# The first item's absolute value on VectorE, and a second scratch buffer for the row maxima

## The chip, the core and the metric

The kernel runs on one core of a Trainium2 chip. A core has five engines, each with its own queue, in order: TensorE (PE, matmuls; its weight loads are listed as PEld), VectorE (DVE), ScalarE (ACT), GpSimd (POOL) and SyncE (SP, which issues most DMAs). The engines wait for each other by semaphores. The metric is the device time of one execution in microseconds (us); lower is better.

## The reference

The input x has 2048 rows of 448 numbers. The output mixes two branches by a gate computed from each row of x:

```python
x = A_u
g = _sigmoid((x * gate_w).sum(-1, keepdims=True))
a = _A_ref(x, ...)     # a long convolution and a skip
b = _B_ref(x, ...)     # attention in 4 segments, 16 heads, with a memory
return g * a + (1 - g) * b
```

The convolution's kernel K is a sum over 256 states of decaying complex exponentials, for each of 448 channels and 2048 positions, and the convolution itself goes through Fourier transforms:

```python
A = -jnp.exp(log_A_real) + 1j * A_imag
C = (C_real + 1j * C_imag) * dt[:, None]
P = jnp.exp((A * dt[:, None])[:, :, None] * pos[None, None, :])
K = 2.0 * jnp.einsum("dn,dnl->dl", C, P).real
```

The attention works in segments of 512 rows, masks what lies ahead of the query, and takes the softmax of the scaled logits; for that each row's maximum is needed:

```python
logits = jnp.einsum("bhqd,bhkd->bhqk", qs, ks) * scale + mask
p = _softmax(logits, axis=-1)
```

## The kernel before

Two halves follow each other. The **first half** builds the convolution's kernel (`first_half`), and beside it projects x to queries, keys and values and transforms x. The **second half** (`second_half`) does the attention, the convolution in the Fourier domain and the output.

In the first half the 448 channels are 28 blocks of 16, and each block has two items, n = 0 to 55. Four items make a group; the groups are numbered 0 to 13 here. For each item:

- `turns(n)`: eight matmuls on TensorE write an angle, in turns, to the PSUM tile `ps_arg` (128x1024; two buffers). These are the rows `ps_arg<-ct,lh` and `ps_arg<-mag,one`.
- `trig(n)`: ScalarE reads that angle twice, once by `Sin` into one half of the tile `cs` and once by `Abs` into the other half; a second `Sin` with a bias then turns the absolute value into the cosine, in place.
- `product(n)`: VectorE multiplies these with decays: X (L392) needs the cosine, Y (L396, L397, L398) the sine.
- `sums(n)`: 64 small matmuls on TensorE add the products up in `ps_k`; after four items VectorE copies `ps_k` to `kb` (L419).

After a group's fourth item come `decays`: six exponentials on ScalarE for the next group (EY and EX, from matmuls `ps_arg<-ce,lh`). Sine and exponential need different function tables, so ScalarE loads a table twice in each group (ACT_TABLE_LOAD). From a sine table load to the next exponential one is called a sine stretch here.

The work beside it, the **feed**, is a generator of steps: matmuls `ps_m<-xh,w` (projections), `ps_m<-wvh,xh` (values), `ps_m<-ut,s1u` (transform of x) and others, with their copies `hi`, `lo`, `am`, `pkT`, `v`, `gs` on ScalarE or VectorE. `feed.spend(us)` issues steps until their stated costs reach the given time; what is over or missing is carried on. A group's rate stands in `RATES`; an item spends 1.7 times the rate, and the places among the six exponentials spend `PLACE` times it. While the exponentials run, the feed's copies are made on VectorE, else on ScalarE. In the sine stretches and beside them VectorE and ScalarE keep the order in which the code issues their main operations (`k.strict`, `follow`); TensorE keeps its program order throughout.

In the second half there are 16 blocks of four heads. For each, `maxima(i)` goes through six steps: matmuls write logits to `ps_mx` (one buffer of 128x2x512), and VectorE then runs `tensor_tensor_reduce`, which adds the mask `mk` and takes the maximum of a row. It writes the masked logits to a scratch tile `jk` that nobody reads, and the maximum, by a short instruction that reads the accumulator, to `mx`. A step has two or four of these, 16 in a block, 256 in all. `jk` had one buffer; the tile `rcb` in `divide` has the same tag, thus the same memory.

What sets the order around both places, in a few lines:

```python
        if n % 4 < 3:
            turns(n + 1)
        trig(n)
        feed.spend(1.7 * RATES[n // 4])
        product(n)
        if n % 4 > 0:
            sums(n - 1)
        if n % 4 == 3 and n + 1 < 2 * NJ:
            decays(n // 4 + 1)
            turns(n + 1)
```

Of the kernel before, what the change touches and what calls it, by code (L numbers as in the profile page):

```python
# [12 lines left out]
F32 = mybir.dt.float32  # L13
F32R = mybir.dt.float32r
BF16 = mybir.dt.bfloat16
I32 = mybir.dt.int32
AF = mybir.ActivationFunctionType
ALU = mybir.AluOpType
# [9 lines left out]
SEG = 512  # L28
# [279 lines left out]
def first_half(nc, k, gy, feed):  # L308
# [4 lines left out]
    act, v = k.act, nc.vector  # L313
# [16 lines left out]
    def load(J):  # L330
        if J < NJ:
            load_decay(J)
            load_phase(J)
# [26 lines left out]
    def turns(n):  # L360

        J, c = divmod(n, 2)
        arg[n] = pt = k.ps("arg")
        for nt in range(2):
            r, kw = rows(nt)
            k.mm(pt[:, nt], lt[J][r, c], k.ct[r, 0], start=True, stop=False, **kw)
        for i in range(2):
            for nt in range(2):
                r, kw = rows(nt)
                k.mm(pt[:, nt], k.one[r], k.mag[r, i : i + 1].broadcast_to([64, 512]), start=False, stop=False, **kw)  # L370
        for nt in range(2):
            r, kw = rows(nt)
            k.mm(pt[:, nt], lt[J][r, c], k.ct[r, 1], start=False, stop=True, **kw)

    def trig(n):

        pt = arg.pop(n)
        cs[n] = t = gw.tile([128, 2, 2, 2, 256], F32, tag="cs", name="cs", bufs=2)
        pv = pt.rearrange("p t (w c) -> p t w c", w=2)
        act(t[:, 1].rearrange("p w t c -> p t w c"), pv, AF.Sin, scale=TWO_PI)  # L380
        act(t[:, 0].rearrange("p w t c -> p t w c"), pv, AF.Abs)
        fl = t[:, 0].rearrange("p w t c -> p (w t c)")
        act(fl, fl, AF.Sin, bias=k.bhp, scale=-TWO_PI)

# [36 lines left out]
    def decays(g):  # L421
        for J in (2 * g, 2 * g + 1):
            for blk in range(3):
# [3 lines left out]
                if g > 0:  # L427
                    k.exps = 3 * (J % 2) + blk >= 2
                    feed.spend(PLACE[3 * (J % 2) + blk] * RATES[g])
                    k.exps = False  # L430
# [7 lines left out]
    for n in range(2 * NJ):  # L438
        if n < 4:
            load(n + 2)  # L440
        elif n % 2 == 0:
            load(n // 2 + 4)
        if n % 4 < 3:
            turns(n + 1)
        trig(n)
        feed.spend(1.7 * RATES[n // 4])
        product(n)
        if n == 2 * NJ - 1:
            feed.fill(2)
# [5 lines that stand above are left out]
# [3 lines left out]

PLACE = (1.24, 0.62, 0.62, 0.62, 0.0, 0.62)

RATES = (1.65, 1.65, 1.24, 1.55, 1.55, 1.17, 1.17, 1.48, 1.55, 1.17, 1.17, 1.48, 1.48, 1.65)


class Feed:
# [482 lines left out]
def attend(nc, k, ap):  # L947

    v, act = k.dve, k.sca.activation
# [32 lines left out]
    def maxima(i):  # L982


        q, kk = Q[i], K[i]
        mx = ap.tile([128, 4, 4], F32, tag="mx", name="mx", bufs=2)
        for b, hp in MSTEPS:
            pt = k.ps("mx")
            for t, o, n in PLACES[b]:
                qt = 3 - t  # L990
                for x in range(2):
                    h = 2 * hp + x
                    r = slice(32 * h, 32 * h + 32)
                    k.mm(
                        pt[:, x, o : o + n], q[r, 0, 128 * qt : 128 * qt + 128], kk[r, 0, :n],
                        start=True, stop=True, tile_position=(32 * h, 0),
                    )
            for t, o, n in PLACES[b]:
                for x in range(2):
                    h = 2 * hp + x  # L1000
                    junk = ap.tile([128, SEG], F32, tag="jk", name="jk", bufs=1)
                    v.tensor_tensor_reduce(
                        junk[:, :n], pt[:, x, o : o + n], k.mk[:, SEG - n :], 1.0, -3e38,
                        ALU.add, ALU.max, mx[:, h, 3 - t : 4 - t],
                    )
            yield
        yield
        pm = k.ps("m")
        k.tr(pm[:16, :128], mx.rearrange("p h t -> p (h t)"), k.ident)
        mn = ap.tile([16, 128], F32R, tag="mn", name="mn", bufs=2)  # L1010
        act(mn, pm[:16, :128], AF.Copy, scale=-1.0)
        k.pdma(
            q[:, 0].rearrange("(j e) (t c) -> e j t c", e=32, c=128)[28].bitcast(F32),
            mn.bitcast(F32),
        )
        yield
# [174 lines left out]
    def divide(hg):  # L1191

        o = pvss[3][:, hg]
        pb = k.ps("m")
        k.mm(pb, k.den, o, start=True, stop=True)
        rc = ap.tile([128, SEG], F32, tag="jk", name="rcb", bufs=1)
        x = None
        for h in range(2):
            c = slice(256 * h, 256 * h + 256)
            with k.issue_after(x.ins) if x else ExitStack():  # L1200
                v.reciprocal(rc[:, c], pb[:, c])
            v.scalar_tensor_tensor(o[:, c], o[:, c], k.omg[:, hg : hg + 1], rc[:, c], ALU.mult, ALU.mult)
            x = v.tensor_tensor(o[:, c], o[:, c], am[3][:, hg, c], ALU.add)
# [461 lines left out]
```

## Time and profile before

| | us |
|---|---|
| three runs | 852.44, 861.59, 861.74 |
| their median | 861.59 |
| the profiled execution | 857.84 |
| its span, first to last instruction | 855.5 |

The span is what the profile's times are counted in, from its start. Engine rows in the profile give the start, the time, the engine, the line (of a helper, where one records all operations: L1377 and L1423), the operation, output<-input, and in brackets how long the engine sat idle before it and what ended this. A wait row gives who waited for whom: us in total, times, longest. A group row gives busy time in all, mean ns of one, and the idle time before. TensorE's ends are modelled, so its busy time is an upper bound of its work. The granted clock of TensorE was 0.946 of full speed in the mean.

### The profile page before, as it was taken

The numbers are of one execution on the slowest core, as the hardware profiler recorded it, in microseconds if no ns is written. First come the engines' busy times: TensorE is split into PE (matmuls) and PEld (weight loads), VectorE is DVE, ScalarE is ACT, GpSimd is POOL, SyncE is SP. The second block draws the span as 40 slices with busy tenths as digits, with TensorE's granted clock in tenths as the row PEclk, the third lists the DMA queues.
The fourth block names the chain that finished last, engine by engine and source line by source line (L and its number), as shares of the span: only waits on it lengthen the run. The fifth ranks groups of instructions, "written<-read, shape, count | busy, mean of one in ns | idle before, by whom it ended". The sixth has DMA issues, their size and how long they took to land.

```text
span 855.5 us, 19160 instructions
## 1 busy us (share of the span) xinstructions
PE 720.8 (84%) x7678; PEld 393.9 (46%) x7703; DVE 581.3 (68%) x1139; ACT 519.6 (61%) x626; POOL 157.2 (18%) x193
## 2 busy tenths in 40 slices
PE   1687988998989988799987787879988798878897
PEld 1364655764556655566643343334433344333333
DVE  8878678867787577976675556558556765662564
ACT  4877889798988899998862144445236333430220
POOL 5324111011100111001100021123114113220110
PEclk9998999998989999999996699999999999988999
DMA  9347853325642346314558769675849577535883
GB/s 247 90 111 240 238 185 111 97 92 164 199 131 79 124 143 206 134 51 143 185 190 290 271 214 277 208 263 155 317 157 317 181 239 239 173 121 225 208 247 117
DMA packets 92450, 157.84 MB, mean 185 GB/s; under 512 B 23074, under 2 KB 60442, under 8 KB 92362
## 3 DMA queue, kind: packets, MB, share of 16 engines
q1 hardware_dynamic: 88410, 153.91, 55.7%
q10 hardware_dynamic: 3072, 1.84, 0.8%
q8 instruction: 61, 1.00, 0.5%
q0 software_dynamic: 880, 0.87, 0.3%
q14 instruction: 27, 0.22, 0.1%
HBM read 88.38 MB, written 60.24 MB: 174 GB/s over the span
## 4 chain that ended last, share of the span: by engine, by line
PE 49%; DVE 17%; ACT 16%; issue 8%; DMA 6%; SPq 2%; POOL 1%; DVEq 0%; ACTq 0%; POOLq 0%
PE ps_m L1423 15%; PE ps_pv L1423 8%; PE ps_c L1423 7%; ACT cs L1377 7%; PE ps_w L1423 6%; DVE jk L1377 6%; PE ps_mx L1423 5%; PE ps_arg L1423 4%; PE ps_k L1423 3%; DVE Y L396 2%; ACT L1377 2%; PE ps_m L1426 2%; DVE pr L1377 2%; DVE Y L397 1%; DMA winv<-in_B_wv 1%
## 5 line engine op out<-in xcount | busy, mean ns | idle before, releaser
L1377 DVE CUSTOM_DVE_ANT_0 jk<-ps_mx,mk 128x512 f32<-128x512 f32 (+3 forms) x256 | 125.4, 490 | 81.5 <-PE ps_mx L1423 72.7
L1377 ACT ACTIVATE PT<-ps_w 128x1024 f32<-128x1024 f32 (+1 forms) x96 | 84.6, 881 | 151.5 <-PE ps_w L1423 150.7
L358 POOL TENSOR_TENSOR EX<-EX,cab 128x1024 f32<-128x1024 f32 x28 | 53.9, 1928 | 311.1 <-ACT EX L1377 267.6
L1377 ACT ACTIVATE cs<-ps_arg 128x1024 f32<-128x1024 f32 x111 | 107.3, 1021 | 3.0 <-DVE Y L397 2.5
L1423 PE MATMUL ps_m<-xh,w 112*128 112x512 f32 x256 | 92.8, 412 | 1.0 <-DMA w<-WD 0.5
L1045 POOL TENSOR_SCALAR_AFFINE_SELECT PT<-PT 128x256 f32<-128x256 f32 (+1 forms) x96 | 46.6, 485 | 243.5 <-ACT PT L1377 243.4
L1423 PE MATMUL ps_w<-qu,ku 32*128 32x512 f32 (+3 forms) x768 | 87.1, 344 | 2.8 <-ACT PT L1377 2.5
L392 DVE TENSOR_TENSOR X<-EX,cs 128x1024 f32<-128x1024 f32 x56 | 70.7, 1262 | 24.9 <-ACT cs L1377 24.7
L1423 PE MATMUL ps_k<-Y,X 128*32 128x64 f32 x3584 | 64.8, 227 | 10.7 <-DVE Y L397 10.7
L1423 PE MATMUL ps_mx<-ku,qu 32*128 32x512 f32 (+3 forms) x256 | 47.6, 409 | 30.1 <-DVE mx L1377 27.7
L1423 PEld LDWEIGHTS ps_k<-Y,X 128*32 128x32 f32 x3584 | 55.5, 114 | 37.8 <-DVE Y L397 17.7
L396 DVE TENSOR_TENSOR Y<-EY,cs 128x1024 f32<-128x1024 f32 x56 | 69.1, 1234 | 0.0
L1423 PEld LDWEIGHTS ps_w<-qu,ku 32*128 32x128 f32 x768 | 60.0, 186 | 13.2 <-issue 6.1
L1377 ACT ACTIVATE cs<-cs,bhp 128x1024 f32<-128x1024 f32 x56 | 64.4, 1151 | 1.8
L1377 ACT ACTIVATE EY<-ps_arg 128x1024 f32<-128x1024 f32 x52 | 53.2, 1030 | 12.9 <-PE ps_arg L1423 11.8
L398 DVE SCALAR_TENSOR_TENSOR Y<-EY,cs 128x512 f32<-128x512 f32 x56 | 40.5, 723 | 29.6 <-ACT cs L1377 29.0
L1423 PEld LDWEIGHTS ps_m<-xh,w 112*128 112x128 f32 x256 | 48.0, 188 | 20.3 <-issue 7.7
L1423 PEld LDWEIGHTS ps_mx<-ku,qu 32*128 32x128 f32 x256 | 22.6, 193 | 70.6 <-DVE mx L1377 51.9
L1423 PE MATMUL ps_pv<-wz 128*128 128x512 bf16 x137 | 48.4, 407 | 3.6 <-ACT pvs L1377 3.1
L1423 PE MATMUL ps_m<-xl,w 112*128 112x512 f32 x128 | 50.2, 392 | 0.0
L1423 PE MATMUL ps_arg<-ct,lh 64*128 64x512 bf16 x224 | 43.0, 389 | 8.1 <-ACT cs L1377 5.7
L1423 PEld LDWEIGHTS <-lh 64*128 64x128 bf16 x392 | 21.8, 95 | 51.2 <-issue 38.6
(215 smaller groups left out, 1324.7 us busy)
## 6 DMA issues: line engine op xcount, KB each, us to landing
w<-WD SPq DMA_DIRECT2D x32, 448.0 KB, 4.4
qu<-QD SPq DMA_DIRECT2D x16, 512.0 KB, 5.6
ku<-KD SPq DMA_DIRECT2D x16, 512.0 KB, 9.9
GU<-gs SPq DMA_DIRECT2D x32, 224.0 KB, 3.4
GK<-gs SPq DMA_DIRECT2D x8, 896.0 KB, 4.6
gk<-GK SPq DMA_DIRECT2D x16, 448.0 KB, 4.5
gu<-GU SPq DMA_DIRECT2D x16, 448.0 KB, 3.7
ks<-ks SPq DMA_DIRECT2D x32, 224.0 KB, 4.3
```

The lines of the kernel that those rows point to most:

```text
L358: nc.gpsimd.tensor_tensor(o, o, cab, ALU.mult)
L392: v.tensor_tensor(X, ex, t[:, :, 0], ALU.mult)
L396: v.tensor_tensor(Y[:, :, :, :32], lo, y[:, :, :, ::-1], ALU.mult)
L397: v.tensor_tensor(Y[:, 0, :, 32:], ey[:, :, 32:], y[:, 0], ALU.mult)
L398: v.scalar_tensor_tensor(Y[:, 1, :, 32:], ey[:, :, 32:], -1.0, y[:, 1], ALU.mult, ALU.mult)
L1045: nc.gpsimd.affine_select(sl, sl, pat, ALU.is_ge, 0.0, base=0, channel_multiplier=-1)
L1377: x = op(*args, **kw)
L1423: tc.keep_in_program_order(nc.tensor.matmul(*args, **kw))
L1426: tc.keep_in_program_order(nc.tensor.transpose(*args))
```

## The change

The absolute value of each group's first item (n % 4 == 0) is made on VectorE: the sign bit is masked off by a bit operation on the angle in PSUM, and VectorE's instruction is issued ahead of ScalarE's sine. The other three items keep `Abs` on ScalarE. The feed is dealt anew: the fourth item of a group spends 2.5 times the rate where the others spend 1.7, and the rates are other numbers. The scratch tile `jk` gets two buffers, and so does `rcb`, which shares its tag.

```diff
@@ trig
         pv = pt.rearrange("p t (w c) -> p t w c", w=2)
+        if n % 4 == 0:
+            v.tensor_scalar(
+                t[:, 0].rearrange("p w t c -> p t w c").bitcast(I32), pv.bitcast(I32), 0x7FFFFFFF, None, ALU.bitwise_and
+            )
         act(t[:, 1].rearrange("p w t c -> p t w c"), pv, AF.Sin, scale=TWO_PI)
-        act(t[:, 0].rearrange("p w t c -> p t w c"), pv, AF.Abs)
+        if not (n % 4 == 0):
+            act(t[:, 0].rearrange("p w t c -> p t w c"), pv, AF.Abs)
         fl = t[:, 0].rearrange("p w t c -> p (w t c)")
         act(fl, fl, AF.Sin, bias=k.bhp, scale=-TWO_PI)
@@ the loop over items
-        feed.spend(1.7 * RATES[n // 4])
+        feed.spend(ITEMS[n % 4] * RATES[n // 4])
@@ the tables
+ITEMS = (1.7, 1.7, 1.7, 2.5)
+
-RATES = (1.65, 1.65, 1.24, 1.55, 1.55, 1.17, 1.17, 1.48, 1.55, 1.17, 1.17, 1.48, 1.48, 1.65)
+RATES = (1.65, 1.58, 1.19, 1.49, 1.49, 1.12, 1.2, 1.42, 1.45, 1.12, 1.12, 1.42, 1.32, 1.47)
@@ maxima
-                    junk = ap.tile([128, SEG], F32, tag="jk", name="jk", bufs=1)
+                    junk = ap.tile([128, SEG], F32, tag="jk", name="jk", bufs=2)
@@ divide
-        rc = ap.tile([128, SEG], F32, tag="jk", name="rcb", bufs=1)
+        rc = ap.tile([128, SEG], F32, tag="jk", name="rcb", bufs=2)
```

How it moves instructions is seen at three places. The line numbers after the change are 5 higher in and behind `trig`, and 7 higher further down (L1377 becomes L1384). The first place is ScalarE's queue where group 4 begins, before (each row: line, operation, output<-input, and in brackets the queues whose semaphores it waits for):

```order
L1377 ACTIVATE EX<-ps_arg 128x1024 [waits DVE_49,PE_49,Pool_49]
L1377 ACT_TABLE_LOAD
L1377 ACTIVATE cs<-ps_arg 128x2x2x256 [waits PE_49]
L1377 ACTIVATE cs<-ps_arg 128x2x2x256
L1377 ACTIVATE cs<-cs,bhp 128x1024 [waits Activation_49]
L1377 ACTIVATE v_207<-ps_m 128x16x28 [waits PE_49]
```

The same place of ScalarE's queue after the change:

```order
L1384 ACTIVATE EX<-ps_arg 128x1024 [waits DVE_49,PE_49,Pool_49]
L1384 ACT_TABLE_LOAD
L1384 ACTIVATE cs<-ps_arg 128x2x2x256 [waits DVE_49]
L1384 ACTIVATE cs<-cs,bhp 128x1024
L1384 ACTIVATE v_207<-ps_m 128x16x28 [waits PE_49]
```

The absolute value is gone from ScalarE. The sine, which waited for TensorE, now waits for VectorE (for the absolute value, which itself waits for TensorE), and the cosine no longer waits for a result of ScalarE.

The second place is VectorE's queue at the start of group 5, before (`gs` are the feed's copies of transformed x, `kb` the copy of the finished sums, `lo` and `ph` parts of a projection):

```order
L788 SCALAR_TENSOR_TENSOR ph<-ps_m,e 128x512
L775 SCALAR_TENSOR_TENSOR lo<-ps_m,po,hi 128x512
L1377 COPY gs<-ps_m 128x448 x2
L419 COPY kb<-ps_k 128x8x64
L398 SCALAR_TENSOR_TENSOR Y<-EY,cs 128x16x32
L392 TENSOR_TENSOR X<-EX,cs 128x1024
```

The same place of VectorE's queue after the change:

```order
L795 SCALAR_TENSOR_TENSOR ph<-ps_m,e 128x512
L782 SCALAR_TENSOR_TENSOR lo<-ps_m,po,hi 128x512
L1384 COPY gs<-ps_m 128x448
L424 COPY kb<-ps_k 128x8x64
L1384 COPY gs<-ps_m 128x448
L381 TENSOR_SCALAR cs<-ps_arg 128x2x2x256
L403 SCALAR_TENSOR_TENSOR Y<-EY,cs 128x16x32
L397 TENSOR_TENSOR X<-EX,cs 128x1024
```

The absolute value stands ahead of the first product, and one of the two `gs` copies has moved behind `kb`, just ahead of it. Groups 9 and 10 show the same move.

The third place is VectorE's queue at the start of group 6, before (`am` is a copy of what is recalled from the memory):

```order
L1377 COPY gs<-ps_m 128x448 [waits DMAHW4_49,PE_49]
L1377 COPY gs<-ps_m 128x448 [waits DMAHW6_49,PE_49]
L419 COPY kb<-ps_k 128x8x64 [waits PE_49]
L398 SCALAR_TENSOR_TENSOR Y<-EY,cs 128x16x32 [waits Activation_49]
L392 TENSOR_TENSOR X<-EX,cs 128x1024 [waits Activation_49,Pool_49]
```

The same place of VectorE's queue after the change:

```order
L1384 COPY gs<-ps_m 128x448 [waits DMAHW7_49,PE_49]
L424 COPY kb<-ps_k 128x8x64 [waits PE_49]
L1384 COPY am<-ps_m 128x512 [waits PE_49]
L381 TENSOR_SCALAR cs<-ps_arg 128x2x2x256 [waits PE_49]
L403 SCALAR_TENSOR_TENSOR Y<-EY,cs 128x16x32 [waits Activation_49]
L397 TENSOR_TENSOR X<-EX,cs 128x1024 [waits DVE_49,Activation_49,Pool_49]
```

Here a copy `am`, which ScalarE made before, has come to VectorE, between `kb` and the absolute value, and X now waits for VectorE's own absolute value too. In the second half the order of VectorE, ScalarE, GpSimd and TensorE is as before, and so are the names of the semaphores that the maxima wait for: each of the 160 that follow another directly waits for one of VectorE's own results, with one buffer for that of the maximum just ahead, with two for the one before it.

## The prediction

> **What bounds the kernel now.** I read the page's busy times and its chain first, then a table of windows cut at ScalarE's table loads, then the timeline at the points where the edits act, and last the waits.
>
> ```profile
> PE 720.8 (84%) x7678; PEld 393.9 (46%) x7703; DVE 581.3 (68%) x1139; ACT 519.6 (61%) x626; POOL 157.2 (18%) x193
> PE 49%; DVE 17%; ACT 16%; issue 8%; DMA 6%; SPq 2%; POOL 1%; DVEq 0%; ACTq 0%; POOLq 0%
> ```
>
> No engine bounds the whole: half of the chain is TensorE, and VectorE and ScalarE share a third. So each stage needs its own look. In the first half (to about 444 us) every group of four items begins with a sine stretch, from the sine table load to the exponential one. Five such stretches (columns: length, then busy us of each engine, then granted clock, DMA share, GB/s):
>
> ```profile
> core 0: us, PE busy (x) PEld busy (x) DVE busy (x) ACT busy (x) POOL busy (x), PEclk, DMA share, GB/s
> 144.55:159.77 15.22, 14.10 (x204) 10.22 (x200) 11.69 (x17) 14.36 (x16) 1.91 (x1) 1.00 0.09 18
> 174.66:189.61 14.95, 14.62 (x195) 9.85 (x195) 10.72 (x14) 14.79 (x16) 1.91 (x1) 1.00 0.39 129
> 200.44:217.51 17.07, 15.21 (x182) 9.44 (x181) 11.79 (x15) 15.36 (x17) 1.91 (x1) 0.80 0.30 102
> 227.41:244.51 17.10, 15.23 (x182) 9.35 (x181) 11.78 (x15) 15.37 (x18) 1.91 (x1) 0.80 0.41 138
> 312.39:327.70 15.31, 12.27 (x182) 7.55 (x181) 11.45 (x15) 15.15 (x18) 1.91 (x1) 1.00 0.33 106
> ```
>
> In group 9 (312.39) ScalarE is busy 15.15 of 15.31 us and TensorE only 12.27: ScalarE bounds it. In group 4 (174.66) both are full, 14.79 and 14.62 of 14.95, so less ScalarE work alone would hardly shorten it. Group 5 (200.44) has the same 182 matmuls as group 9, but at a granted clock of 0.80 it takes 1.76 us longer; group 6 (227.41) likewise. VectorE has 3 to 4 us free in each.
>
> **Edit 1: the first item's absolute value on VectorE.** The start of group 4:
>
> ```profile
> 173.25 1.03 DVE L419 COPY kb<-ps_k 128x512 f32<-128x512 f32 x1 [2.44 <-PE ps_k L1423]
> 174.00 0.38 PE L1423 MATMUL ps_arg<-ct,lh 64*128 64x512 bf16 x2
> 174.66 1.28 ACT L1377 ACT_TABLE_LOAD   x1
> 175.96 1.94 ACT L1377 ACTIVATE cs<-ps_arg 128x1024 f32<-128x1024 f32 x2
> 177.93 1.15 ACT L1377 ACTIVATE cs<-cs,bhp 128x1024 f32<-128x1024 f32 x1
> 179.18 1.23 DVE L392 TENSOR_TENSOR X<-EX,cs 128x1024 f32<-128x1024 f32 x1 [1.47 <-ACT cs L1377]
> L1377 ACT ACTIVATE cs<-ps_arg 128x1024 f32<-128x1024 f32 x111 | 107.3, 1021 | 3.0 <-DVE Y L397 2.5
> ```
>
> Sine and Abs are the pair at 175.96, the cosine starts at 177.93, 1.97 us behind the sine. The pair takes 1.94 us and one of them 1.02 us, so an independent second one starts 0.92 us behind the first. After the change the cosine follows the sine without a wait on ScalarE itself (the order shows none), so I put it 0.92 us behind: 1.05 us less on ScalarE in each group. ScalarE also gets a new wait: the sine stands behind VectorE's absolute value. Queued behind that sine are the cosine, the copies am, pkT or v, and the next item. So the gain is 1.05 us less the lateness of the sine.
>
> The absolute value reads 128x1024 from PSUM; VectorE did not do that before. Nearest rows:
>
> ```profile
> L1377 DVE COPY gs<-ps_c 128x896 f32<-128x896 f32 x8 | 8.7, 1091 | 15.5 <-PE ps_c L1423 10.4 <-issue 4.6 <-PE ps_mx L1423 0.5
> L1377 DVE COPY gs<-ps_m 128x448 f32<-128x448 f32 x13 | 8.0, 619 | 2.7 <-PE ps_m L1423 2.7
> ```
>
> 472 ns for 448 more columns is 1.05 ns a column; 128 more than 896 give 1.23 us. Bounds: 1.09 us (the 896 row) below and 2.46 us (half that speed, a bit operation being unseen here) above; I take 1.23, nearest to the copies. A handover is 0.10 us (the cosine ends at 179.08, X starts at 179.18). So VectorE needs to be free, and the first angle ready, 1.33 us ahead of the sine's old start. In group 4 both are so by 174.38 (173.25 + 1.03, and 174.00 + 0.38), 1.58 us ahead: hidden behind the table load. Elsewhere a copy stands later on VectorE:
>
> ```profile
> 117.09 0.68 DVE L1377 COPY pkT<-ps_m 128x512 f32<-128x512 f32 x1
> 118.91 1.94 ACT L1377 ACTIVATE cs<-ps_arg 128x1024 f32<-128x1024 f32 x2
> 144.44 0.67 DVE L1377 COPY pkT<-ps_m 128x512 f32<-128x512 f32 x1
> 145.84 1.94 ACT L1377 ACTIVATE cs<-ps_arg 128x1024 f32<-128x1024 f32 x2
> 199.03 1.03 DVE L419 COPY kb<-ps_k 128x512 f32<-128x512 f32 x1 [0.65 <-PE ps_k L1423]
> 201.74 1.94 ACT L1377 ACTIVATE cs<-ps_arg 128x1024 f32<-128x1024 f32 x2
> 256.48 0.69 DVE L1377 COPY am<-ps_m 128x512 f32<-128x512 f32 x1
> 257.84 1.94 ACT L1377 ACTIVATE cs<-ps_arg 128x1024 f32<-128x1024 f32 x2
> 89.41 0.69 DVE L773 TENSOR_TENSOR lo<-ps_m,hi 128x512 fp32r<-128x512 f32 x1
> 90.16 1.94 ACT L1377 ACTIVATE cs<-ps_arg 128x1024 f32<-128x1024 f32 x2
> ```
>
> Group 2: 117.77 + 1.33 is 0.19 us late, gain 0.86. Group 3: 145.11 + 1.33, 0.60 late, gain 0.45. Groups 7 and 11 (row of 7): 257.17 + 1.33, 0.66 late, gain 0.39 each. In groups 5, 9 and 10 the new order puts one gs copy (0.62 us) behind kb: 200.06 + 0.62 + 1.33, 0.27 late, gain 0.78 each. Group 6 gets an am copy (0.69 us) there: gain about 0.71. Together 5.1 us. Groups 4 and 8: 1.05 us on ScalarE, but TensorE idles only 0.33 us there: 0.4 us each, 0.8 together. Group 1: 90.10 + 1.33 is 1.27 late, a loss of 0.2 us. Groups 0, 12 and 13 I have not worked out (other work stands ahead of the sine there); they and group 1 are set to zero together. Term: 5.9 us. Bounds: 14 x 1.05 = 14.7 us; at an absolute value of 2.46 us, a loss of about 5 us.
>
> The Trainium skill, "PSUM — Partial Sum Buffer", section "Terms", says that no two engines may access the same bank in the same partition at once, reads among them. The order agrees with that page, since the sine waits for VectorE; without that wait the eight groups would give 8 x 1.05 = 8.4 us and not 5.1.
>
> **The feed dealt anew.** TensorE's matmuls are the same. With ITEMS and RATES a group is dealt 11.32 times its rate, against 10.52 before: in group 1 17.9 and not 17.4 us. The order shows few steps that change their stretch: parts of six or three matmuls go from before a sum to behind it, values matmuls go behind the last exponent, one projection part (six matmuls) goes from group 12 into 13. TensorE is in order, so this moves work within the same TensorE time: nothing. SP's issues of GU, ut and lh change places with it; by the code most are issued a group ahead of their use, and if that cover were gone TensorE would wait as here:
>
> ```profile
> 441.56 2.30 PE L1423 MATMUL ps_m<-ut,s1u 64*128 64x448 f32 x4 [0.81 <-DMA ut<-in_A_u]
> ```
>
> At this end of the first half the order has one transform step and two ut loads fewer left: 0.8 us gained, between 0 and 2.
>
> **Edit 2: two buffers for jk.** In the second half VectorE:
>
> ```profile
> 716.37 0.69 DVE L1377 CUSTOM_DVE_ANT_0 jk<-ps_mx,mk 128x512 f32<-128x512 f32 x1
> 716.99 0.08 DVE L1377 DVE_READ_ACCUMULATOR2_ANT mx<- 128x1 f32 x1
> 717.10 0.69 DVE L1377 CUSTOM_DVE_ANT_0 jk<-ps_mx,mk 128x512 f32<-128x512 f32 x1
> 717.72 0.08 DVE L1377 DVE_READ_ACCUMULATOR2_ANT mx<- 128x1 f32 x1
> 717.72 0.74 DVE L1377 SCALAR_TENSOR_TENSOR am<-am,gh,ps_m 128x512 f32<-128x512 f32 x1
> ```
>
> The second jk starts 0.11 us behind the read of the accumulator (716.99 to 717.10), while the am operation, which writes elsewhere, starts with such a read (both 717.72). With one buffer each later maximum waits for the write of the one ahead; with two it waits for the one before that, long done. So 0.11 us goes per maximum that follows another directly. There are 160 of these (10 in each of 16 blocks), 17.6 us of VectorE's time; what counts is where the chain passes through them and on to TensorE:
>
> ```profile
> PE ps_mx L1423 <- DVE mx L1377: 27.7, 25, 2.5
> 459.99 0.69 DVE jk L1377
> 767.83 0.29 DVE jk L1377
> ```
>
> The chain holds 68 such followers, these two the first and the last: 68 x 0.11 = 7.5 us. Some of it meets a TensorE that waits for another operand next, so I take three quarters, 5.6 us; bounds 0 and 17.6. The buffer rcb only shares the tag; its two reciprocals write halves of one tile: nothing.
>
> **Sum.** 5.9 + 0.8 + 5.6 = 12.3 us. The profiled execution took 857.84 us (span 855.5): 845.5. The three runs (852.44, 861.59, 861.74) and this one have a mean of 858.4, 0.6 above it, and the median shown lies 3.75 above it. I add 0.6: 846 us.
>
> **Rivals.** (a) *The wait of jk costs nothing by itself*: the 0.11 us is the maximum's own end, and the next one needs it with any buffer. For it: no row shows two maxima without the wait. Against it: the am operation at 717.72. The second term falls away: 852 us. The Trainium skill, "VectorE: DVE Perf Modes", section "The DRAIN you can't avoid", measured eight copies with and without semaphores at the same time and says the semaphore costs nothing extra. By that page this rival holds; the two starts at 717.72 speak against the page.
>
> (b) *The absolute value comes too late*: VectorE's copies wait for TensorE in more groups than here, and the first term is nil. For it: 0.60 and 0.66 us of lateness already; against it: groups 2, 4 and 8. 857.84 - 6.4 + 0.6 = 852 us.
>
> (c) *More comes*: the waits of TensorE behind the first cosine shrink, and the slow clock of groups 5 and 6 does not appear. The 1.76 us between the two windows above, twice, and the full 7.5 us: 857.84 - 5.9 - 0.8 - 3.5 - 7.5 + 0.6 = 841 us.
>
> (d) *Slower*: the absolute value takes 2.46 us. The eight groups then lose 8 x 0.59 = 4.7 us in place of gaining 5.1; TensorE waits at the same place, and groups 9 and 10 get the clock of group 5, 3.5 us; with (a) that gives 867 us. It decides at 1.23 + 5.1/8 = 1.87 us: above this the first half loses. Against it: X, 1024 columns from two operands, takes 1.23 us in its row above.
>
> **Chances.** Forecast 0.54, its own range 841 to 851; (a) 0.14; (b) 0.11; (c) 0.16; (d) 0.05. The range 838 to 856 holds all but (d) and the ends. Faster by over 2% is below 844.4 us (2% is about what a measurement of this kernel can tell from no change): (c) and a fifth of the forecast, 0.27. Slower by over 2% is above 878.8 us: less than (d), 0.02. The rest is within: 0.71.
>
> **What would show it.** Right: 42 cs<-ps_arg on ScalarE and 14 on VectorE near 1.23 us; sine stretches of groups 5, 9 and 10 shorter by 0.6 to 0.8 us and of 4 and 8 by less than 0.5; a jk starting with the read ahead of it; less of TensorE's wait on mx than 27.7 us. Wrong: jk still 0.11 us behind the read (a); sines that start more than 0.7 us behind the table load's end (b); a VectorE operation above 1.87 us (d); another place where the saved time turns into a new wait.

## The result and the profile after

| us | before | after |
|---|---|---|
| median | 857.77 (20 runs, 848.23 to 869.35) | 844.21 (20 runs, 823.37 to 851.43) |
| mean | 857.6 | 839.9 |
| profiled execution, span | 857.84, 855.5 | 833.71, 832.0 |

The ratio is 0.9696, its 95% interval 0.9656 to 0.9737: faster. It leaves out the runs of either kernel that lie over 1.5% above that kernel's fastest, of the changed kernel all thirteen from 840 us up. The means of all runs differ by 17.8 ± 2.4 us (2.1%), the medians by 13.6 us (1.6%). The changed kernel's runs fall into two groups, seven from 823 to 836 us at a mean granted clock of 0.962 to 0.977 and thirteen from 840 to 851 us at 0.923 to 0.954. The profiled execution is one of the first group (0.962; before 0.946), so its 24 us are not the change alone.

The page's busy times and its chain, after:

```profile
PE 707.3 (85%) x7678; PEld 388.8 (47%) x7703; DVE 584.7 (70%) x1154; ACT 503.1 (60%) x611; POOL 156.2 (19%) x193
PE 58%; DVE 16%; ACT 13%; issue 6%; DMA 5%; SPq 1%; POOL 1%; ACTq 0%; DVEq 0%; POOLq 0%
```

TensorE has the same 7678 matmuls, and is busy 13.5 us less: with no matmul removed, that is shorter matmuls. The clock fits this: the clock records have 63 us at half speed after and 93 before. Its share of the chain went from 49 to 58%. ScalarE has 16.5 us less, of which the 14 absolute values make 14.3 (14 x 1.02).

The absolute values and the first item of group 5, by the groups and the timeline after (the bracket is the idle time before the row and what ended it):

```profile
L381 DVE TENSOR_SCALAR cs<-ps_arg 128x1024 int32<-128x1024 int32 x14 | 17.1, 1223 | 6.6 <-PE ps_arg L1430 6.6
200.98 0.62 DVE L1384 COPY gs<-ps_m 128x448 f32<-128x448 f32 x1
201.85 1.22 DVE L381 TENSOR_SCALAR cs<-ps_arg 128x1024 int32<-128x1024 int32 x1 [0.24 <-PE ps_arg L1430]
203.10 1.02 ACT L1384 ACTIVATE cs<-ps_arg 128x1024 f32<-128x1024 f32 x1 [0.47 <-DVE cs L381]
204.02 1.14 ACT L1384 ACTIVATE cs<-cs,bhp 128x1024 f32<-128x1024 f32 x1
```

The operation takes 1.22 us, the sine waits 0.47 us for it, and the cosine starts 0.92 us behind the sine. The sine waits so in all 14 groups, by 0.42 to 2.12 us behind the end of the table load, and in nine of them by more than the 0.7 us that the prediction named as a sign of its rival (b). Group 4, where the prediction had it hidden:

```profile
175.84 1.28 ACT L1384 ACT_TABLE_LOAD   x1
175.85 0.39 PE L1430 MATMUL ps_arg<-ct,lh 64*128 64x512 bf16 x2
176.94 1.23 DVE L381 TENSOR_SCALAR cs<-ps_arg 128x1024 int32<-128x1024 int32 x1 [1.60 <-PE ps_arg L1430]
178.19 1.03 ACT L1384 ACTIVATE cs<-ps_arg 128x1024 f32<-128x1024 f32 x1 [1.07 <-DVE cs L381]
```

VectorE is free here and waits for the angle: the angle's first matmul starts with the table load, where before the change it started 0.66 us ahead (174.00 and 174.66), since values matmuls of the feed now stand in front of it. In ten of the 14 groups VectorE waits so, 6.6 us in all (the group row above).

Two maxima in a row, by VectorE's timeline after:

```profile
692.81 0.68 DVE L1384 CUSTOM_DVE_ANT_0 jk<-ps_mx,mk 128x512 f32<-128x512 f32 x1
693.42 0.09 DVE L1384 DVE_READ_ACCUMULATOR2_ANT mx<- 128x1 f32 x1
693.42 0.69 DVE L1384 CUSTOM_DVE_ANT_0 jk<-ps_mx,mk 128x512 f32<-128x512 f32 x1
```

The next maximum starts with the read of the accumulator, and not 0.11 us behind it. So do all 160 that follow another, where all 160 of the kernel before start 0.11 to 0.12 us behind it. The third set of rows is windows of the changed kernel: the exponential stretches behind groups 3 and 7, then the sine stretches of groups 4, 5 and 9 (columns as in the prediction's first table):

```profile
162.28:175.84 13.56, 13.09 (x181) 9.26 (x179) 8.66 (x15) 9.86 (x12) 1.92 (x1) 1.00 0.44 140
268.02:280.91 12.89, 12.89 (x181) 9.31 (x179) 8.63 (x15) 9.94 (x12) 1.91 (x1) 1.00 0.47 149
175.84:191.17 15.33, 14.83 (x202) 9.91 (x202) 12.44 (x15) 13.81 (x15) 1.91 (x1) 1.00 0.39 126
201.35:216.05 14.70, 12.54 (x185) 7.74 (x181) 12.94 (x17) 14.11 (x16) 1.91 (x1) 1.00 0.37 121
306.57:321.27 14.70, 12.53 (x185) 7.70 (x182) 12.93 (x17) 14.11 (x16) 1.91 (x1) 1.00 0.40 136
```

The same two exponential stretches before:

```profile
159.77:174.66 14.89, 14.15 (x191) 9.86 (x188) 8.59 (x15) 10.09 (x12) 1.92 (x1) 1.00 0.39 128
271.73:286.62 14.89, 14.15 (x191) 9.86 (x188) 8.61 (x15) 10.10 (x12) 1.92 (x1) 1.00 0.41 129
```

They lost ten matmuls each (191 to 181) and 1.33 and 2.00 us. The prediction did not look at them. The sine stretch of group 4 has seven matmuls more (195 to 202) and is 0.38 us longer, although one absolute value less stands in it on ScalarE. Group 5 now runs at a clock of 1.00 and takes as long as group 9.

### The profile page after: what moved, and what is told of

It is laid out like the page before. It is cut to its first block, busy times and chain, and to the rows that moved or that the text cites. A ratio compares the mean times of both kernels' runs of the same rounds, so it can differ in the third digit from the quotient of the medians.

```text
span 832.0 us, 19142 instructions
## 1 busy us (share of the span) xinstructions
PE 707.3 (85%) x7678; PEld 388.8 (47%) x7703; DVE 584.7 (70%) x1154; ACT 503.1 (60%) x611; POOL 156.2 (19%) x193
## 4 chain that ended last, share of the span: by engine, by line
PE 58%; DVE 16%; ACT 13%; issue 6%; DMA 5%; SPq 1%; POOL 1%; ACTq 0%; DVEq 0%; POOLq 0%
PE ps_m L1430 21%; PE ps_pv L1430 8%; PE ps_c L1430 7%; PE ps_w L1430 6%; PE ps_arg L1430 5%; ACT cs L1384 5%; PE ps_mx L1430 5%; PE ps_k L1430 4%; DVE jk L1384 4%; DVE Y L401 2%; DVE pr L1384 1%; PE ps_m L1433 1%; DVE cs L381 1%; DVE Y L402 1%; ACT gs L1384 1%
## 5 line engine op out<-in xcount | busy, mean ns | idle before, releaser
L1384 ACT ACTIVATE PT<-ps_w 128x1024 f32<-128x1024 f32 (+1 forms) x96 | 84.6, 881 | 149.6 <-PE ps_w L1430 148.7
L1384 DVE CUSTOM_DVE_ANT_0 jk<-ps_mx,mk 128x512 f32<-128x512 f32 (+3 forms) x256 | 112.7, 487 | 81.9 <-PE ps_mx L1430 76.8
L1384 ACT ACTIVATE cs<-ps_arg 128x1024 f32<-128x1024 f32 x97 | 94.5, 1023 | 13.0 <-DVE cs L381 10.9
L1430 PE MATMUL ps_k<-Y,X 128*32 128x64 f32 x3584 | 62.5, 222 | 14.5 <-DVE Y L402 14.4
L1430 PEld LDWEIGHTS ps_k<-Y,X 128*32 128x32 f32 x3584 | 53.3, 111 | 39.8 <-DVE Y L402 26.1
L1430 PE MATMUL ps_mx<-ku,qu 32*128 32x512 f32 (+3 forms) x256 | 46.0, 396 | 24.8 <-DVE mx L1384 22.2
L1384 ACT ACTIVATE cs<-cs,bhp 128x1024 f32<-128x1024 f32 x56 | 64.3, 1149 | 1.4
L1384 ACT ACTIVATE EY<-ps_arg 128x1024 f32<-128x1024 f32 x52 | 52.5, 1036 | 4.4 <-PE ps_arg L1430 4.2
L1430 PEld LDWEIGHTS ps_mx<-ku,qu 32*128 32x128 f32 x256 | 22.2, 190 | 64.1 <-DVE mx L1384 42.4
```

The lines of the kernel that those rows point to most:

```text
L1384: x = op(*args, **kw)
L1430: tc.keep_in_program_order(nc.tensor.matmul(*args, **kw))
```

## The experiments

Each kernel was run beside the kernel before on the same chip. The parts of the first half are told apart by ScalarE's table loads; most stretches whose granted clock is 1.00 repeat to 0.05 us from run to run (those of groups 1 and 13 vary by up to 1.5 us). Half clock is counted from the clock records of the traces, which are 1.0 or 0.5 of full speed at any time. Means are given with their standard errors.

### The control and the three edits alone

The kernel before once more (c0_before_again):

> The kernel before, unchanged, as a control, so that its runs stand with their granted clock beside those of the changed kernels. Every theory: the same as before, ratio 1.00, median 855 to 860 us. Theory 1 (the part of the gain above the predicted 12 us is the granted clock, which differs from run to run): its runs spread over about 20 us and follow the clock, near 855 us of span at a clock of 0.946 and near 845 us at 0.96. Theory 2 (the gain above 12 us belongs to the change): its runs at 0.946 and at 0.96 are no more than 3 us apart.

Ratio 0.9986 (0.9958 to 1.0014), mean 855.4 ± 1.7 beside 855.9 ± 0.9 us for the 35 runs of before. The runs follow the clock in the main: 865 and 866 us at 0.934 and 0.938, 854 at 0.951, 847 at 0.963, but also 852 at 0.939 and 856 at 0.935 (correlation 0.80 over the 47 runs of this program). The spread is 19 us in one program: theory 1, though not as strictly as it was put.

Edit 2 alone (e1_jk_only), the diff's last two places:

> Two buffers for jk and rcb, nothing else. As predicted (0.11 us for each of 160 maxima that follow another, a third of them on the way to the end): 5.6 us less, median near 852 us; the first half as before, the second half 411.5 us before and about 406 now; a second jk starts with the read ahead of it. Rival, the wait costs nothing by itself: 0.1 us between read and next jk as before, no change of time. Rival, all of the second half's 10.3 us in the profile of the changed kernel is jk: second half near 401 us, median near 847 us.

Mean 854.2 ± 2.3, median 855.0 us: 1.7 ± 2.5 us less in the mean, 0.2 us more in the median, so no gain is shown, and 5.6 us are not refuted by this run alone. But the 0.11 us are gone in the trace:

```profile
661.28 0.69 DVE L1377 CUSTOM_DVE_ANT_0 jk<-ps_mx,mk 128x512 f32<-128x512 f32 x1 [1.78 <-PE ps_mx L1423]
661.90 0.08 DVE L1377 DVE_READ_ACCUMULATOR2_ANT mx<- 128x1 f32 x1
661.90 0.69 DVE L1377 CUSTOM_DVE_ANT_0 jk<-ps_mx,mk 128x512 f32<-128x512 f32 x1
```

So the first rival is wrong about the wait. The saved time also reaches TensorE, in the wait that the prediction named as a sign (27.7 us before):

```profile
PE ps_mx L1423 <- DVE mx L1377: 21.3, 22, 2.4
```

In the four profiles here that have two buffers and no dummy matmuls added, this wait is 20.7 to 22.2 us, in the eight with one buffer 26.4 to 27.7. What stands against the gain shows in windows of the whole second half, from the first maximum to the end, of the kernel before and of this one (the column ahead of the DMA share is the granted clock):

```profile
456.30:855.51 399.21, 333.45 (x2520) 150.28 (x2539) 235.55 (x661) 139.46 (x182) 73.49 (x128) 0.93 0.67 221
```

```profile
454.43:858.20 403.77, 347.35 (x2541) 152.29 (x2539) 221.43 (x661) 139.59 (x182) 73.32 (x128) 0.91 0.67 218
```

VectorE is busy 14 us less, the clock is lower, and the half is 4.6 us longer. Half clock is 52.1 us in the first and 73.0 us in the second.

Edit 1 alone (e2_abs_only), the diff's place in `trig`, with the old items and rates:

> The absolute value of each group's first item on VectorE, with the feed's old items and rates and one jk buffer. As predicted: 5.9 us less, median near 852 us; the sine stretches of groups 2, 3, 9 and 10 shorter by 0.5 to 0.9 us at a granted clock of 1.00, those of 4 and 8 by up to 0.4, the exponential stretches within 0.3 us of before. Rival, the edit only pays with the feed dealt anew (VectorE's copies stand ahead of the absolute value): sine stretches within 0.3 us of before, no change of time.

Mean 850.5 ± 1.6 us: 5.4 ± 1.8 less, as predicted. Groups 2 and 3 are shorter by 0.66 and 0.65 us, 9 and 10 by 1.05 and 1.06 and 4 and 8 by 0.45, both a little more than the range named. With the old feed the sine of groups 4, 5, 6, 8, 9 and 10 is not late at all; group 4 here:

```profile
173.54 1.23 DVE L381 TENSOR_SCALAR cs<-ps_arg 128x1024 int32<-128x1024 int32 x1
173.79 1.28 ACT L1382 ACT_TABLE_LOAD   x1
175.09 1.03 ACT L1382 ACTIVATE cs<-ps_arg 128x1024 f32<-128x1024 f32 x1
```

The feed alone (e3_feed_only), the diff's places in the loop over items and in the tables:

> The feed's new items and rates, with the absolute value on ScalarE and one jk buffer. As predicted (work moves within the same TensorE time): nothing but 0.8 us at the end of the first half, median near 857 us. Rival, the feed carries what was missing in the sum: the exponential stretches of groups 3, 4, 7 to 9 and 11 to 13 shorten by 0.5 to 2 us each, 7 to 9 us together, and the time by 4 to 8 us, median near 851 us. Second rival, what leaves the exponential stretches is added to the sine stretches while ScalarE makes the absolute values: the former shorten by 7 to 9 us and the latter lengthen by as much, no change.

Mean 846.3 ± 1.3 us: 9.5 less, the largest of the three, at a higher mean clock (0.953 against 0.945). The first rival is right in kind (6.8 us leave the exponential stretches, where it said 7 to 9). The stretches at a granted clock of 1.00, in us (old code: from e1_jk_only, whose first half is that of before; both: from c1_changed_again below):

| stretch | old code | edit 1 | feed | both |
|---|---|---|---|---|
| sine, group 4 | 14.94 | 14.49 | 15.32 | 15.33 |
| sine, group 5 | 15.29 | 14.24 | 15.31 | 14.70 |
| sine, group 9 | 15.30 | 14.24 | 15.32 | 14.71 |
| sine, sum of groups 2 to 12 | 166.7 | 160.0 | 167.1 | 163.7 |
| exponential, behind group 3 | 14.90 | 14.88 | 13.56 | 13.56 |
| exponential, behind group 7 | 14.89 | 14.89 | 12.88 | 12.84 |
| exponential, sum of groups 3, 4, 5, 7, 8, 9, 11, 12 | 97.2 | 96.9 | 90.4 | 90.3 |
| group 1, both stretches | 28.5 | 28.6 | 29.4 | 29.8 |
| sine, group 13, to the last table load | 21.8 | 21.9 | 20.1 | 20.2 |

By this table edit 1 alone brings 7.0 us (6.7 in the sine stretches, 0.3 in the exponential ones) and the feed alone 7.3 us (6.8 in the exponential stretches, 1.7 at the end, less 0.4 in the sine stretches and 0.8 in group 1). Together they bring 10.2 us, not 14.3: part of what edit 1 frees in the sine stretches is where the feed's work went, and with the new feed the sine waits for the absolute value. On top of the feed, edit 1 is worth 2.9 us. The table leaves out the stretches that ran at half clock in one of these profiles, and its rows on groups 1 and 13 are the loose ones: the last row is 20.8 us in c0_before_again, with the same code as the first column. Why the feed brings anything is seen in windows of this kernel, the exponential stretch behind group 3 and the sine stretches of groups 4 and 9:

```profile
158.50:172.06 13.56, 13.11 (x181) 9.28 (x179) 8.67 (x15) 9.89 (x13) 1.92 (x1) 1.00 0.42 140
172.06:187.38 15.32, 14.82 (x202) 9.90 (x202) 11.20 (x14) 14.83 (x16) 1.91 (x1) 1.00 0.39 126
303.51:318.83 15.32, 12.55 (x185) 7.70 (x182) 11.71 (x16) 15.16 (x17) 1.91 (x1) 1.00 0.38 124
```

In an exponential stretch TensorE is busy nearly all the time (13.11 of 13.56 us, before 14.15 of 14.89) and ScalarE is not (9.89 us); in the sine stretch of group 9 it is the other way round (ScalarE 15.16 of 15.32, TensorE 12.55). A matmul taken from the first shortens it; put into the second it fills a gap. The total of TensorE's work is the same, its price is not.

### Both parts of the feed, and the changed kernel without the second buffer

The changed kernel itself (c1_changed_again):

> The changed kernel, unchanged, as a control beside the next runs. Every theory: mean near 840 us, ratio near 0.97 to 0.98. Theory 1 (the runs differ by where a grid of 3.41 us, on which the clock is set, falls on TensorE's idle places): spans of 820 to 850 us that follow the mean granted clock, near 842 us of span at 0.946, where the kernel before takes near 855. Theory 2 (the times are the change's alone): runs of equal clock differ from the kernel before by over 20 us.

Mean 845.3 ± 1.4, median 846.2 us, 10.2 ± 1.6 us (1.2%) under the kernel before; near 840 us and 2 to 3% were expected. None of its nine runs was under 840 us and none had a clock above 0.952 (0.929 to 0.952), so the 3.0% of the first measurement did not come again. At 0.949 a run took 845 us, and the kernel before, on the same chip, 854 to 859 us at 0.948 to 0.951: theory 1, without the 20 us of theory 2.

The changed kernel with one buffer (e4_abs_and_feed): edit 2 undone.

> The changed kernel with one buffer for jk and rcb: the absolute value and the feed's numbers stay. As predicted for jk (5.6 us): 4 to 8 us slower in the mean than the changed kernel, near 846 us; blocks 0 to 14 of the second half, at equal time of half clock, 5 to 7 us longer together. Rival, jk is worth nothing once the clock is evened out: the mean of the changed kernel, 840 us. First half as in the changed kernel within 3 us.

Mean 842.9 ± 1.0 us, 2.4 ± 1.8 below the changed kernel on the same chip. No gain of the second buffer shows in the time.

Only the fourth item's spend raised (e5_items_only), and only the rates changed (e6_rates_only); of the feed's edit above, the one has the new `ITEMS` with the old `RATES`, the other the new `RATES` with 1.7 for all:

> The kernel before with the fourth item's spend raised to 2.5, the old rates. If the fourth item's larger spend is what moves TensorE's work out of the exponential stretches (where TensorE bounds) into the sine stretches (where it idles): the exponential stretches of groups 3, 7 and 9 shorten as with the whole new feed (1.3, 2.0, 0.5 us), mean near 848 us. Rival, it is the rates: these stretches stay within 0.3 us of before, since places and rates are as before.

> The kernel before with the new rates, all items at 1.7. If the fourth item's spend is what matters: less is dealt in every group (about 4% less), so the rest of the feed comes behind the last item and the end of the first half grows by 3 to 8 us, with the exponential stretches shorter by at most 0.3 us: mean 856 to 864 us. Rival, the lower rates alone empty the exponential stretches: they shorten by 4 to 7 us together, mean near 851 us.

Mean 862.1 ± 0.8 (6.6 slower) and 864.6 ± 0.7 us (9.1 slower): each part alone makes it worse, both together make it better. The first table of windows is e5_items_only, the sine stretch of group 3 and the exponential one behind it; the second is e6_rates_only, the last sine stretch:

```profile
147.84:166.89 19.05, 17.93 (x262) 12.76 (x262) 15.27 (x21) 14.89 (x17) 1.91 (x1) 1.00 0.14 37
166.89:178.48 11.59, 11.22 (x146) 7.59 (x135) 5.18 (x10) 9.80 (x12) 1.92 (x1) 1.00 0.41 147
```

```profile
418.90:444.86 25.96, 23.93 (x344) 14.76 (x341) 20.80 (x26) 18.68 (x23) 1.92 (x1) 1.00 0.57 191
```

With the items alone 3.30 us leave the exponential stretch (before 14.89) and 3.83 come into the sine stretch (15.22), which got 58 matmuls more (204 to 262), more than its gaps hold. With the rates alone less is dealt, and the rest lies behind the last item: 25.96 us there and not 21.8. The exponential stretches shorten there too (13.04 us behind group 3; the eight of the table above 89.3 us, 7.9 less, as the rival for the rates had it), but the sine stretches of groups 2 to 12 grow by 13.6 us to 180.3, three of them at half clock in part. So the first theory for the items was wrong in its sum, and the first for the rates was near in the time (864.6 where 856 to 864 was expected) and wrong about the stretches. The gain is one of amounts: it comes as long as the gaps of the sine stretches hold what is moved.

### Where the second buffer's gain went

Between blocks of the second half that had the same time of half clock, the second buffer does shorten them: block 2, at full clock, took 11.92 us with one buffer and 11.15 with two, block 7 17.34 and 16.98, block 9 16.98 and 16.53, though block 8 took 30.76 with either. Ten profiles (the kernel before, c0, e1, e2, e3, e4 and e12, the changed kernel three times) follow a line with a residual of 1.3 us: length of the second half = 378.6 us, less 5.9 ± 1.0 us with two buffers, plus 0.40 us for each us of half clock (0.51 without the last profile of the changed kernel, which fell on its slowest run, 862 us). The half clock itself: 52.1, 52.1, 66.0, 52.0, 52.2 and 65.7 us with one buffer (mean 56.7), 45.8, 66.2, 73.0 and 107.6 us with two (mean 73.1). 16.4 x 0.40 = 6.6 us: on these means all of the 5.9 us is given back. But the four with two buffers scatter so far (standard error 13 us) that their mean alone does not show more half clock. From the start of block 14 to the end they do: 32 to 38 us in the four, 11 to 34 in the six with one buffer, means 36.6 and 20.7, a difference of 15.9 ± 3.5 us.

The runs bear this out in part. Over the three pairs without dummy matmuls added (e1_jk_only with the kernel before, c1 with e4, c2 with e12) two buffers are 1.0 ± 1.4 us slower in the weighted mean, so the time does lack the gain. But the granted clocks of all these runs make 5.7 ± 4.2 us more half clock with two buffers, and to take back 5.9 us at 0.40 would need 15. So by the ends of the profiles the clock takes back all of it, and by the clocks of whole runs about 2 us (5.7 x 0.40); which of the two holds is not settled.

What brings half clock shows where the clock changes. Here are windows of the kernel before, on the grid of its clock records (to 0.06 us); the first three are at the start of the sine stretch of group 5, the last three at that of group 9, which has the same matmuls:

```profile
202.57:205.98 3.41, 1.58 (x14) 0.73 (x11) 1.71 (x2) 3.38 (x6) 0.00 (x0) 1.00 0.16 43
205.98:209.40 3.42, 3.42 (x10) 2.07 (x10) 3.38 (x7) 2.82 (x3) 0.00 (x0) 0.51 0.21 79
209.40:212.81 3.41, 3.41 (x73) 2.26 (x73) 3.12 (x4) 3.11 (x4) 0.00 (x0) 0.50 0.35 107
311.80:315.21 3.41, 2.83 (x18) 1.24 (x15) 0.68 (x2) 3.38 (x4) 1.91 (x1) 1.00 0.72 234
315.21:318.62 3.41, 1.83 (x15) 1.13 (x15) 1.94 (x3) 3.38 (x6) 0.00 (x0) 1.00 0.16 57
318.62:322.04 3.42, 3.42 (x79) 2.09 (x78) 3.38 (x6) 3.39 (x6) 0.00 (x0) 1.00 0.08 28
```

The waits in the first of these intervals, by TensorE's timeline of the kernel before:

```profile
203.73 0.39 PE L1423 MATMUL ps_arg<-ct,lh 64*128 64x512 bf16 x2 [0.72 <-ACT cs L1377]
205.88 1.54 PE L1423 MATMUL ps_m<-v,pkT 128*128 128x128 f32 x6 [1.11 <-ACT pkT L1377]
```

The clock changes only on a grid of 3.41 us. In group 5 the waits of TensorE fell into one interval, 1.58 us busy, and the next two ran at half clock; in group 9 the grid lay 0.7 us later against the work, the poorest interval had 1.83 us, and nothing happened. Over the 17 profiles of this study, from 60 us on, 120 of the 122 full-clock intervals with less than 1.5 us of TensorE were followed by half clock, and 12 of the 2901 with over 2.5 us; in between it was a quarter. All 250 returns to full clock followed an interval with at least 2.99 us, but not every such interval brought one (205.98 above). The Trainium skill, "TensorE: Matmul & The Clock Gate", section "What's actually happening", has the same grid (3413 ns, free-running, two levels) and has the slow clock come after an idle window; these runs agree on the grid and show that no idle window is needed: one that is less than half full was enough.

The grid starts anywhere, so the same code meets it differently in each run. At the end of the second half, e1_jk_only and, for the same place, e3_feed_only:

```profile
781.75:785.16 3.41, 1.73 (x5) 0.86 (x5) 1.43 (x2) 0.00 (x0) 0.00 (x0) 1.00 0.18 67
785.16:788.57 3.41, 3.41 (x6) 1.35 (x4) 0.00 (x0) 0.00 (x0) 0.00 (x0) 0.50 0.00 0
```

```profile
771.42:774.83 3.41, 2.58 (x7) 0.97 (x6) 0.68 (x1) 0.00 (x0) 0.40 (x1) 1.00 0.10 38
774.83:778.24 3.41, 2.57 (x8) 1.28 (x8) 0.75 (x1) 0.00 (x0) 0.00 (x0) 1.00 0.18 67
```

The two waits in the first pair, by TensorE's timeline of e1_jk_only:

```profile
782.76 0.50 PE L1423 MATMUL ps_m<-r,sel 8*128 8x512 f32 x1 [0.83 <-DVE tb L1377]
784.10 4.97 PE L1423 MATMUL ps_m<-wo,pvs 128*128 128x448 f32 x8 [0.84 <-DVE am L1377]
```

Both kernels have here the same two waits, 0.83 us for VectorE's tb and 0.84 for am; in e1_jk_only both fall into one interval, in e3_feed_only into two.

To test whether such waits bring the half clock, dummy matmuls were put in. First one more at each step of blocks 1 to 15 that has some already (e7_more_turns):

```diff
-                    turn_over(1 if r < 3 else 2)
+                    turn_over(2 if r < 3 else 3)
```

> The changed kernel with one more dummy matmul of 512 columns (TensorE's own, its result is not read) in front of each of the steps of the second half that already have one or two, 75 in all, 0.21 us each at full clock. If low activity of TensorE is what brings the half clock: less half clock in the second half (46 to 66 us before), by 10 us or more, and the time falls by up to 5 us against the changed kernel. Rival, the dummies cost more than they bring, since most places have work waiting: up to 75 x 0.21 = 16 us slower.

Half clock in the second half is 37.5 us in its profile, less than in any other but one (the profile fell on the fastest of its four runs); mean 842.7 ± 1.6 us, within the errors of the changed kernel's 845.3, which was on another chip. So half clock is less where TensorE has more to do, as far as one profile shows it, and the dummies cost time of their own: block 7, without half clock in both, took 17.69 us and not 16.97.

Then three of them only at the waits for tb and am (e8_fill_end), and the same with one buffer (e9_fill_end_one_jk):

```diff
+            if t > 0:
+                k.fill(3)
             out_mm(s, t, po[:, :D], range(4))
             store(s, t, po[:, :D], xts[t])
             if t > 1:
+                k.fill(3)
                 next(memory)
```

> The changed kernel with three dummy matmuls (0.64 us at full clock) at the places of blocks 13 to 15 where TensorE waits 0.83 to 0.85 us for VectorE's tb and am, and at the like places of the two earlier segment ends. Theory: the second jk buffer's 6 us are given back at the end of the second half, because the saved time lets TensorE's idle places fall into one interval of the clock's 3.41 us grid; with the idle places filled, half clock from the start of block 14 to the end falls from 38 to 20 us or less, and the mean is 4 to 8 us below the changed kernel's, 837 to 841 us beside 845. Rival, the half clock there is a matter of other waits: as much of it, same time within 2 us.

> The kernel of the run before (the changed one with filled waits) with one buffer for jk and rcb. If the end's half clock ate the second buffer's gain: now, with the waits filled, one buffer is 4 to 7 us slower than two (without the filling it was no slower: 842.9 against 845.3 us in the mean). Rival, the second buffer is worth nothing on the way to the end: within 2 us of the run before.

Half clock from block 14 on fell from 38 to 21 us, and the mean to 838.8 ± 0.7, 6.5 below c1, though on another chip. Blocks 8 and 12 grew by 1.7 us each. With one buffer the mean is 851.6 ± 1.4: 12.9 ± 1.6 slower, more than the 5.9 us of the second buffer by itself. The two profiles differ by 3.8 us in the first half, where the code is the same, so clock is in this difference too; how much was not settled.

The last four ran on one chip, with the filling kept to the last segment's end (`if s == 2`): e10_fill_last_segment, the same with one buffer, the changed kernel and the changed kernel with one buffer.

> The kernel with filled waits, but the dummy matmuls only at the last of the three segment ends (blocks 13 to 15). At the two earlier ones they made blocks 8 and 12 1.66 us longer each, since TensorE had other work there. Theory: 3.3 us less than with all three filled, so 835 to 837 us in the mean, where the changed kernel has 842 to 845. Rival, the grid falls elsewhere and takes it back: 838 to 842 us.

> The run before with one buffer for jk and rcb. If the second buffer's own worth (6 us in blocks 0 to 14 at equal half clock) reaches the end when the last waits are filled: 4 to 8 us slower than the run before. Rival, its worth is decided by the place of the clock's grid alone: between 3 us faster and 13 us slower, the two differences seen so far.

> The changed kernel once more, on the chip of the three runs beside it. Mean 840 to 846 us; half clock from the start of block 14 to the end 28 to 38 us as in its two profiles so far.

> The changed kernel with one buffer for jk and rcb once more, on the same chip as the changed kernel. If the second buffer is worth nothing to the end: within 2.5 us of the changed kernel, either way (842.9 against 845.3 in the first pair). If its 6 us come through: 4 to 8 us slower.

| | two buffers | one buffer |
|---|---|---|
| last waits filled | 837.9 ± 2.7 | 845.8 ± 2.7 |
| as the change has it | 845.0 ± 3.9 | 843.2 ± 2.0 |

Without the filling, two buffers are not faster than one, for the second time (1.7 ± 4.3 us slower here, 2.4 ± 1.8 in the first pair). With it they are 8.0 ± 3.8 us faster, which both theories of e11 allow. The kernel with two buffers and the last waits filled has the lowest mean of all, 20.2 ± 2.9 us under the kernel before, but that it beats the changed kernel (7.1 ± 4.7 us) is not shown.

## Why the prediction was right or wrong

It said 846 us, range 838 to 856, and gave 0.71 to a change within 2%. The median, 844.21, lies in the range; the measured 3.0% is twice the 1.4% that was forecast (12.3 of 857.84 us). Over three sets of runs (20, 9 and 7) the changed kernel's mean lies 17.8 ± 2.4, 10.2 ± 1.6 and 13.1 ± 4.0 us under that of the kernel before beside it, 15.0 when weighted by runs; the sum said 12.3. That the sum comes so near is luck: it lacked a gain in the first half and held one in the second that did not reach the time, and the two nearly cancel.

**The feed: the step that failed.** "TensorE is in order, so this moves work within the same TensorE time: nothing." The matmuls are the same, but the time is not the sum of TensorE's work: an exponential stretch is nearly as long as TensorE's work in it, a sine stretch like that of group 9 nearly as long as ScalarE's. Moving work from the one to the other gained 6.9 us in the exponential stretches of the changed kernel, and the feed alone 7.3 us in all. Half of the reason was in the prediction, TensorE busy 12.27 of 15.31 us in group 9; the exponential stretches' rows were not looked at. The end of the first half, 0.8 us by the prediction, gained 0.6 to 1.6 us. Group 1, set to zero, lost 0.1 to 1.7 us in the profiles of the new code that ran it at full clock.

**The absolute value: the durations right, the lateness not.** It took 1.223 us where 1.23 was taken; the cosine comes 0.92 us behind the sine; the handover to ScalarE takes 0.03 us where 0.10 was taken. Alone the edit brought 7.0 us by stretches and 5.4 ± 1.8 in the mean; the term said 5.9. On top of the new feed it brings 2.9 us. The prediction read the lateness of the sine from the kernel before, as if the feed left the angle where it was. In the changed kernel the sine of groups 4 and 8, which were to hide it behind the table load, is 1.07 and 1.25 us late, and that of groups 5 and 9 0.47 and 0.48 where 0.27 was taken. The sign of rival (b) thus came true in nine groups, in group 4 by a wait for TensorE's angle and not for VectorE's copies; (b) itself, a term of nil, did not. Groups 5 and 9 came out 0.59 us shorter and not 0.78, group 7 0.19 and not 0.39, and groups 4 and 8 0.39 and 0.54 us longer where 0.4 less was forecast. (Three smaller slips: the 42 operations cs<-ps_arg that were to stay on ScalarE are the absolute values alone, with the 56 sines there are 98; by its rows VectorE had 3.5 to 5.3 us free in the five sine stretches, not 3 to 4; and rival (d) left out the 0.8 us of the end, so its 867 would be 866.)

**Two buffers for jk: the size right, the way to the end wrong.** 5.6 us were predicted. TensorE's wait for the maxima fell by as much (26.4 to 27.7 us with one buffer, 20.7 to 22.2 with two), and 5.9 us were found at equal half clock; rival (a), that the wait costs nothing, is refuted by the starts at 693.42. But the prediction treated the time saved in a block as time saved at the end. Without dummy matmuls the three pairs with and without the second buffer show no gain (1.0 ± 1.4 us slower). At the end of the second half the profiles with two buffers have 15.9 ± 3.5 us more half clock, which is 6.4 us at 0.40; over whole runs the granted clocks show less half clock than that. That the cause is TensorE's waits falling together on the grid rests on the intervals and on the fillings; whether the clock takes back all of it, and why two buffers meet the grid worse at the end in all four profiles, stays open.

**The slow clock.** Rival (c) had it that the slow clock of groups 5 and 6 would not appear. In the profile after it did not, and in no profile of the changed kernel; but e1_jk_only, with the first half of before, shows it as little: it is a matter of where the grid lies. Over the first twenty runs the kernel met the grid well (seven runs at 0.962 and above), in c1 not once in nine, in c2 twice in seven. By stretches at equal clock the edits are worth 10.2 us in the first half, where 6.7 was predicted, and 5.9 in the second, where 5.6 was. A ratio of 0.9696 makes 26 us of 857.8; that the 10 us beyond these 16 are clock follows by subtraction and was not measured apart. How much of the clock comes by the change and how much by chance, these runs don't settle.

## What to carry to other kernels

Work that moves between stretches has no price of its own: look at what bounds the stretch it leaves and the stretch it comes to, in a table of both, before writing "same work, nothing", and look at what stands behind it in its queue (here an angle that two engines wait for). A gain on an engine that TensorE waits for can be lost again to TensorE's clock, so compare lengths at equal granted clock first, stretch by stretch, and then count the half clock apart. Where runs of one kernel spread by 2%, a single profile's difference is no measure of a change of 1%.

## What was not expected of the hardware

- In these traces TensorE's clock changes between 1.0 and 0.5 on a grid of 3.41 us whose place differs from run to run, and goes with how busy TensorE was in the interval before: half clock after fewer than 1.5 us of 3.41 in 120 of 122 cases, full again only after 2.99 us or more. Waits of 0.7 to 1.1 us were enough where two fell into one interval. A us of half clock cost 0.40 us in the second half by the line through ten profiles.
- A maximum that waits for the write of the one just ahead starts 0.11 to 0.12 us after the start of the accumulator's read (all 160 pairs of the kernel before); without that wait it starts with it (all 160 of the changed kernel, as at 693.42). The Trainium skill, "VectorE: DVE Perf Modes", section "The DRAIN you can't avoid", says that the semaphore costs nothing extra; for this pair of instructions the traces say otherwise.
